# Attention and a gated feed-forward layer on one core: how the first exponentials are turned, who copies the early results, and where the first matmul groups end

## The chip, the cores and the metric

The program runs on one core of one Trainium2 chip. The metric is the device time of an execution in microseconds (us). The kernel before took 466.61 us, the median of three executions (465.33 to 467.41). One more execution was profiled; the profile, its page and every stretch quoted here are of that one.

## The reference

Twelve heads of eight batches, 448 positions of 64 values: a softmax with one more term in its denominator, then a dense layer with Mish between two matrices.

```python
scores = (1 / sqrt(64)) * q @ k.transpose(0, 1, 3, 2)        # 8 x 12 x 448 x 448
m = max(scores, axis=-1)
e = exp(scores - m)
attn = e / (sum(e, axis=-1) + exp(-m) + 1e-09)
x = (attn @ v) as rows of 12 * 64 = 768 values                # 3584 rows
h = x @ w_in                                                  # 768 x 2048
g = h * tanh(log1p(exp(h)))                                   # Mish
out = g @ w_out                                               # 2048 x 768
```

## The kernel before, in words

Two heads make a pair; 8 batches of 6 pairs are 48 pairs, numbered from 0. For a pair, `load_pair` (L133) brings q, k and v, `cast` (L177) makes them bf16 on GpSimd, `transpose_pair` (L207) turns q and k on TensorE into a PSUM bank, and `evac_qk` (L238) copies them to SBUF. `scores` (L309) multiplies in four steps; after each step VectorE takes the negated row maxima (L350, `negm`), and `exps` (L355) lets ScalarE write the exponentials with their sums (L366, `en`). For the second product the exponentials must be turned, `en` to `eT`. `normalise` (L428) issues that as a transposing DMA on SyncE (L440), called T(p) below for pair p. It is cut in four blocks j along the key positions. `turn_on_pe` (L445) turns one block with seven TensorE transposes (L452) and a VectorE copy (L455). `av_pair` (L463) multiplies by v (L480), AV(p) below, and its `evac` copies the result to `xT` (L493 or L495).

The division by the denominator is done in one of two ways. For a pair that `divided` (L108) names, `normalise` multiplies `en` on VectorE by the reciprocal, seven instructions (L432), ahead of T(p). For the others `spread_rden` (L396) spreads the reciprocals over a PSUM bank with 16 small matmuls (L411), a copy makes `rb` of it (L420), and the output is multiplied by it as it leaves PSUM (L495).

The head of the program (L656) does pairs 0 to 5 one after another; pair p's AV follows three pairs later. Then come units of three pairs, u = 2 to 17 (u = 2 is pairs 6 to 8, u = 3 is 9 to 11, u = 4 is 12 to 14, u = 5 is 15 to 17), with two more units without attention at the end. A unit has twelve steps, in which AVs of earlier pairs and parts of the second matrix product (`mm2_part`, L588) are woven between the scores, and then eight passes f = 0 to 7 that do the first matrix product (`mm1_mish`, L532; matmuls L525, Mish L541), turn later q and k, and issue the T of the unit's three pairs in the order of the list `todo` (L784).

Which groups of L525 start early is written out: in u = 2 and 3 `mm1_begin` (L513) starts four groups in the steps; in u = 2 they stop short of the last one or two matmuls, which `mm1_mish` adds in its pass. Pairs 5, 6 and 7 (`BY_PE`, L633) are turned by TensorE wholly and have no T.

All order is by hand; each engine takes its instructions strictly in program order. Four orders matter here. SyncE's queue holds the loads (L140), the T, the turns of later q and k (L202) and the stores (L553). GpSimd's holds the casts and, at L174, the weights' loads: `load_w` (L165) first copies a few values of some pair's `eT` (L169), so it waits until that pair's T has landed: six pieces of `w_in` behind T(4), five pieces behind T(8), four behind the last pair in u = 3. Two PSUM banks, `mo`, are shared by everything that calls `mo_take` (L124). And `flush_late` (L120) puts copies out of PSUM where the next step begins. `eT` has three buffers, so T(p) waits for AV(p-3).

Of the kernel before, what the change touches and what calls it, by code (L numbers as in the profile page):

```python
# [15 lines left out]
UNIT_PAIRS = 3  # L16
# [3 lines left out]
def kernel(  # L20
# [9 lines left out]
    nc = tc.nc  # L30

    B, H, S, D = q.shape
# [3 lines left out]
    NT = 4  # L36
    SP_ = S // NT
    HP = H // 2
    DM_T = d_model // 128
# [5 lines left out]
    FF_U = FF_T // UNITS_PER_B  # L45
# [57 lines left out]
    QB = S // 64  # L103
    DIAG_FROM = 2 * HP
    LATE_DIV = 2 * HP
    EARLY_DIV = (HP, HP + 1, HP + UNIT_PAIRS)

    def divided(p):  # L108
        return p >= LATE_DIV or p in EARLY_DIV
# [10 lines left out]
    def flush_late():  # L120
        while late:
            late.popleft()()
# [42 lines left out]
    def load_w(n, behind=None):  # L165
        if behind is not None:
            i = n_marks[0]
            n_marks[0] += 1
            nc.gpsimd.tensor_copy(  # L169
                out=marks[0:1, i, 0:2], in_=att[behind]["eT"][0:1, NT - 2, 2 * S - 2 : 2 * S]  # L170
            )
        for _ in range(min(n, len(pieces))):
            dst, src = pieces.popleft()
            nc.gpsimd.dma_start(out=dst, in_=src.rearrange("(a p) c -> p a c", p=128))  # L174
# [253 lines left out]
    def normalise(p, dma=True):  # L428
        st = att[p]
        en = st["en"]  # L430
        for i in range(NTILE if divided(p) else 0):
            nc.vector.tensor_scalar(  # L432
                out=en[:, :, i, 0:SP_], in0=en[:, :, i, 0:SP_],
                scalar1=st["rden"][:, i : i + 1], scalar2=None, op0=ALU.mult,
            )
        eT = eT_pool.tile([128, NT, 2 * S], BF16, tag="eT", name="eT")
        st["eT"] = eT
        if dma:
            n = NT - 1 if p < HEAD else NT
            nc.sync.dma_start_transpose(  # L440
                out=eT[:, 0:n, :].rearrange("c j (i q) -> c (j i) q", q=128),
                in_=en[:, 0:n].rearrange("q j i c -> q (j i c)"),
            )

    def turn_on_pe(p, j, busy_first=0):  # L445

        st = att[p]
        own = mo_take()
        keep_busy(busy_first, bank=own)
        ps = own[:, :].bitcast(BF16).rearrange("c (i q) -> c i q", q=128)  # L450
        for i in range(NTILE):
            nc.tensor.transpose(ps[0:SP_, i, :], st["en"][:, j, i, 0:SP_], ident)  # L452

        def evac():
            nc.vector.tensor_copy(  # L455
                out=st["eT"][0:SP_, j, :].rearrange("c (i q) -> c i q", q=128),
                in_=ps[0:SP_, 0:NTILE, :],
            )
            mo_free.append(own)

        late.append(evac)

    def av_pair(p, bank=None, beside=None, half=None, hold=False):  # L463
        b, hp = p // HP, p % HP
        eT = att[p]["eT"]
        v_bf = casted[p]["v"]
        if b not in xT:
            xT[b] = xT_pool.tile([128, DM_T, S], BF16, tag="xT", name="xT")
        if half is not None:
            bank = free_half(half)  # L470
            mms = av_beside.setdefault(half * STEPS + STEPS - 1, [])
        av = mo_take() if bank is None else bank
        for j in range(NT):
            for h in range(2):
                if p >= DIAG_FROM:
                    by_h = eT[0:SP_, j, :].rearrange("c (i h r) -> c h i r", h=2, r=64)
                    e_h = by_h[:, h]
                else:
                    e_h = eT[0:SP_, j, h * S : (h + 1) * S]
                mm = nc.tensor.matmul(  # L480
                    av[h * 64 : (h + 1) * 64, 0:S],
                    lhsT=v_bf[:, h, j * D : (j + 1) * D],
                    rhs=e_h,
                    start=(j == 0), stop=(j == NT - 1),
                )
                if half is not None:
                    apart(mm, half_max[half])
                    mms.append(mm)

        def evac():  # L490
            to = xT[b][:, hp, :]
            if divided(p):
                read = nc.vector.tensor_copy(out=to, in_=av[:, 0:S])  # L493
            else:
                read = nc.vector.tensor_tensor(  # L495
                    out=to, in0=av[:, 0:S], in1=rb.pop(p), op=ALU.mult
                )
            if half in half_exp:
                apart(read, half_exp[half])
            elif beside is not None or half is not None:  # L500
                av_read[beside if half is None else half * STEPS + STEPS - 1] = read
            if bank is None:
                mo_free.append(av)

        if p in spread_copy:
            late.append(spread_copy.pop(p))
        (held if hold else late).append(evac)
        del att[p], casted[p], qkT[p]


    begun = {}

    def mm1_begin(b, ff, upto):  # L513

        bank = mm1_bank(ff)
        begun[b, ff] = (bank, upto)
        mm1(b, ff, bank, 0, upto)

    def mm1_bank(ff, ahead=2):
        at = ff % FF_U - 2  # L520
# [2 lines left out]
    def mm1(b, ff, bank, lo, hi):  # L523
        for dm in range(lo, hi):
            nc.tensor.matmul(  # L525
                bank[:, 0:S],
                lhsT=w_in_sb[:, dm, ff * 128 : (ff + 1) * 128],
                rhs=xT[b][:, dm, :],
                start=(dm == 0), stop=(dm == DM_T - 1),
            )  # L530
# [99 lines left out]
    HEAD = HP  # L630
    BY_DMA_FROM = 2 * HP + 2 * UNIT_PAIRS

    BY_PE = {HEAD - 1: 1, HEAD: -2, HEAD + 1: 2}  # L633
    AV_AT = {0: {1: 3, 5: 4, 8: 5}, 1: {1: 8, 4: 6, 8: 7}}
    RDEN_AT = {0: {0: 3, 2: 4, 5: 5}, 1: {0: 8}, 2: {3: 10, 5: 11}}
    MM1_AT, MM1_SHORT = (6, 7, 9, 10), (2, 1, 1, 1)

    W_AT = ({5: 2}, {1: 3})
# [17 lines left out]
    for p in range(HEAD):  # L656
        for s in range(STEPS):
            exps(p * STEPS + s)
            if s == 0 and p == 0:
                evac_qk(1, act=True)  # L660
            flush_late()
            if s == 1:
                late.extend(held)
                held.clear()
                flush_late()
            if s == 2:
                evac_qk(p + 2, act=p % 2 == 0)
            scores_ahead(HEAD * STEPS + 3)
            if s == 0:
                transpose_pair(p + 2)  # L670
                if p:
                    denominators(p - 1)
            if s == 1 and p:
                turn_on_pe(p - 1, NT - 1)
            if s == 2:
                if p >= 3:
                    spread_rden(p - 3)
                cast(p + 3, "qkv" if p + 3 < HEAD else "qk")
                if p == HEAD - 1:
                    load_w(6, behind=p - 1)  # L680
            if s == 3:
                if p >= 3:
                    av_pair(p - 3, hold=True)
                if p + 5 < 10:
                    load_pair(p + 5, "qkv" if p + 5 <= HEAD else "qk")
                normalise(p, dma=p not in BY_PE)
            if s < 3:
                keep_busy(2, half=p)
    denominators(HEAD - 1)

    for u in range(UNITS_PER_B, N_UNITS + 2 * UNITS_PER_B):
# [5 lines left out]
        p0 = u * UNIT_PAIRS  # L697
        if attn and u >= first_mm2:
            av_with.update({p0 + i: p0 + i - UNIT_PAIRS for i in range(UNIT_PAIRS)})
        nxt = p0 + UNIT_PAIRS  # L700
        end = min(nxt, N_PAIRS) * STEPS

        for n in range(steps):
            pi, s = divmod(n, STEPS)
            p, idx = p0 + pi, p0 * STEPS + n
# [46 lines left out]
            for pe, n0 in BY_PE.items():  # L752
                j = n - n0
# [29 lines left out]
        b, w = (u - UNITS_PER_B) // UNITS_PER_B, u % UNITS_PER_B  # L783
        todo = sorted(range(p0, nxt), key=lambda p: p in BY_PE)  # L784
        if u == UNITS_PER_B + 1:
            todo = [p0 + 1, p0, p0 + 2]
        for f in range(FF_U):
            if moe:
                mm1_mish(b, w * FF_U + f)
            if u == UNITS_PER_B and f == 3:  # L790
                load_w(5, behind=p0 + 2)
            if u == UNITS_PER_B + 1 and f == FF_U - 1:
                load_w(4, behind=p0 + 2)
            if not attn:
                continue
            if f == 0:
                denominators(p0, UNIT_PAIRS)
                for p in todo[:2] if p0 < LATE_DIV else todo[:1]:
                    normalise(p, dma=p not in BY_PE)
            if f in (1, 3, 5):  # L800
                if nxt < BY_DMA_FROM:
                    transpose_pair(nxt + f // 2, bank=f // 2 % 2)
                    evac_qk(nxt + f // 2)
            if f == 1 and p0 < LATE_DIV:
                normalise(todo[2], dma=todo[2] not in BY_PE)
            if f == FF_U - 1:
                scores_ahead(min(nxt * STEPS + len(sc_tiles), N_PAIRS * STEPS))
            if f in (3, 5) and p0 >= LATE_DIV:
                p = todo[1 + f // 5]
                normalise(p, dma=p not in BY_PE)  # L810
    flush_late()
# [31 lines left out]
```

## Time and profile before

| | |
|---|---|
| median of three executions | 466.61 us |
| profiled execution, device time | 465.31 us |
| its span, first to last instruction | 463.5 us |
| mean granted TensorE clock | 0.993 |
| TensorE matmuls busy | 443.5 us, 96% |
| VectorE busy | 346.9 us, 75% |
| ScalarE busy | 331.4 us, 72% |
| GpSimd busy | 184.3 us, 40% |
| DMA moved | 97.93 MB, mean 211 GB/s |

The page cuts the span into 40 equal slices and gives each engine's busy share as a digit; a second part follows the chain of work that ended last; a third lists groups of instructions with the busy time, the mean of one, and the idle time before them with what ended it. "<-" reads "made from" in a name and "released by" after an idle time. Stretches give the busy time of each engine between two moments, then the granted clock, the DMA engines' busy share (above 1 where packets of two queues are under way on the same engine) and the rate. A DMA's time to landing counts from its issue to its last write.

### The profile page before, as it was taken

To read this page: it belongs to the slowest core of one execution; us is meant where nothing else is said; L and a number is where in the kernel's file an instruction comes from. 1 tells how busy PE (TensorE), PEld (TensorE's weight loads), DVE (VectorE), ACT (ScalarE), POOL (GpSimd) and SP (SyncE) were. 2 spreads that over 40 slices of the span, in tenths; PEclk is the share of its full clock that TensorE was granted. 3 is DMA by queue.
4 is the path that set the end of the run, shared out by engine and by line. 5 is a ranking of instruction groups with operands and counts; after the bars stand their busy time and mean duration, and the time that the engine had idled before them with its cause. 6 is when DMAs were issued, how large, how long until landed. Compare 5 with 4: busy or idle time off the path is not lost.

```text
span 463.5 us, 8735 instructions
## 1 busy us (share of the span) xinstructions
PE 443.5 (96%) x2991; PEld 243.9 (53%) x2991; DVE 346.9 (75%) x670; ACT 331.4 (72%) x874; POOL 184.3 (40%) x267
## 2 busy tenths in 40 slices
PE   6788989999999999999999999999999999999996
PEld 3344555555555555555555555555555555556563
DVE  5989969688798898989898979989888979311021
ACT  5999878898797878787887968787878779221300
POOL 4434648043346271736464643727363610100000
PEclk9989999999999999999999999999999999999999
DMA  8999999999999999999989999999999392911122
GB/s 245 243 213 233 223 215 229 190 238 246 235 262 275 239 252 218 283 211 263 256 275 242 267 219 231 260 231 247 258 272 235 113 243 76 245 62 35 34 69 68
DMA packets 232492, 97.93 MB, mean 211 GB/s; under 512 B 189312, under 2 KB 228992, under 8 KB 232448
## 3 DMA queue, kind: packets, MB, share of 16 engines
q1 hardware_dynamic: 224928, 91.06, 83.1%
q0 software_dynamic: 7488, 6.29, 8.6%
q8 instruction: 23, 0.38, 0.3%
q14 instruction: 21, 0.17, 0.1%
q10 hardware_dynamic: 32, 0.02, 0.0%
HBM read 45.61 MB, written 11.01 MB: 122 GB/s over the span
## 4 chain that ended last, share of the span: by engine, by line
PE 71%; ACT 14%; DVE 11%; issue 2%; DMA 0%; SPq 0%; DVEq 0%; ACTq 0%
PE mo L525 26%; PE mo L588 24%; ACT en L366 11%; DVE negm L350 8%; PE sc L329 8%; PE sc L480 6%; PE sc L525 4%; PE sc L290 1%; DVE eT L455 1%; PE sc L335 1%; DVE xT L493 1%; PE mo L480 1%; ACT L541 1%; PE sc L225 1%; ACT kT_all L280 0%
## 5 line engine op out<-in xcount | busy, mean ns | idle before, releaser
L366 ACT ACTIVATE en<-sc,negm 128x448 bf16<-128x448 f32 x336 | 209.3, 640 | 29.7 <-DVE negm L350 28.0
L350 DVE TENSOR_REDUCE negm<-sc 128x2 f32<-128x896 f32 x192 | 180.4, 969 | 42.3 <-PE sc L329 32.0
L588 PE MATMUL mo<-w_out_sb,gT 128*128 128x384 bf16 (+1 forms) x1024 | 166.7, 306 | 0.4 <-DVE rb L420 0.4
L525 PE MATMUL mo<-xT,w_in_sb 128*128 128x448 bf16 x660 | 132.2, 352 | 1.0 <-ACT gT L541 0.5
L588 PEld LDWEIGHTS <-gT 128*128 128x128 bf16 x1024 | 96.3, 98 | 56.0 <-issue 1.9
L270 POOL TENSOR_SCALAR qd<-qT_all 64x448 bf16<-64x448 bf16 x60 | 79.8, 1330 | 90.4 <-DMA qT_all<-q_cast 61.9
L525 PEld LDWEIGHTS <-w_in_sb 128*128 128x128 bf16 x768 | 74.2, 98 | 69.7 <-issue 3.9
L541 ACT ACTIVATE gT<-mo 128x448 bf16<-128x448 f32 x110 | 58.2, 543 | 68.9 <-PE mo L525 68.7
L432 DVE TENSOR_SCALAR en<-en,rden 128x448 bf16<-128x448 bf16 x273 | 87.1, 394 | 0.6
L366 ACT ACTIVATION_READ_ACCUMULATOR en<-sc,negm 128x1 f32 x336 | 71.0, 211 | 0.0
L571 DVE COPY o_sb<-mo 128x384 f32<-128x384 f32 (+1 forms) x64 | 31.9, 498 | 49.8 <-PE mo L588 49.0
L329 PE MATMUL sc<-kT_all,qd 128*128 128x448 bf16 x252 | 67.6, 354 | 0.0
L480 PE MATMUL sc<-eT,v_bf 112*64 112x448 bf16 x336 | 39.8, 357 | 1.6 <-ACT en L366 1.1
L329 PEld LDWEIGHTS <-qd 128*128 128x128 bf16 x252 | 24.6, 98 | 28.7 <-issue 12.9
L191 POOL CAST q_cast<-q_f 112x512 bf16<-112x512 f32 x47 | 28.7, 610 | 5.5 <-DMA q_f<-in_q_dram 5.4
L480 PEld LDWEIGHTS <-v_bf 112*64 112x64 bf16 x384 | 20.1, 109 | 20.1 <-issue 12.6
L191 POOL CAST k_cast<-k_f 112x512 bf16<-112x512 f32 x47 | 28.6, 609 | 0.7 <-DMA k_f<-in_k_dram 0.4
L191 POOL CAST v_bf<-v_f 112x512 bf16<-112x512 f32 x48 | 28.1, 607 | 1.3 <-DMA v_f<-in_v_dram 0.9
L735 POOL COPY marks<-en 1x2 bf16<-1x2 bf16 x12 | 2.1, 174 | 64.2 <-DVE en L432 64.2
L525 PE MATMUL sc<-xT,w_in_sb 128*128 128x448 bf16 x108 | 23.4, 353 | 1.4 <-ACT gT L541 1.4
L493 DVE CAST xT<-sc 128x448 bf16<-128x448 f32 x36 | 22.1, 615 | 0.0
L541 ACT ACT_TABLE_LOAD x14 | 18.0, 1283 | 0.8 <-PE mo L525 0.6
(63 smaller groups left out, 238.8 us busy)
## 6 DMA issues: line engine op xcount, KB each, us to landing
k_f<-in_k_dram SPq DMA_DIRECT2D x48, 224.0 KB, 5.1
q_f<-in_q_dram SPq DMA_DIRECT2D x48, 224.0 KB, 4.9
v_f<-in_v_dram SPq DMA_DIRECT2D x48, 224.0 KB, 5.0
w_in_sb<-in_moe_w_in_dram POOLq DMA_DIRECT2D x12, 256.0 KB, 9.8
w_out_sb<-in_moe_w_out_dram POOLq DMA_DIRECT2D x8, 384.0 KB, 13.7
out_dram<-o_sb SPq DMA_DIRECT2D x7, 336.0 KB, 3.4
out_dram<-o_sb SPq DMA_DIRECT2D x8, 288.0 KB, 4.8
out_dram<-o_sb SPq DMA_DIRECT2D x8, 240.0 KB, 3.4
```

The costliest lines, as they stand in the source:

```text
L191: nc.gpsimd.tensor_copy(out=to[nm], in_=src)
L270: q_reads.append(by.tensor_scalar(out=qd[rows, :, h, :], in0=q_ps[rows, 0:S].rearrange("d (i r) -> d i r", i=QB), scalar1=SCALE, scalar2=N ...
L329: nc.tensor.matmul(sc[:, bk, 0:S], lhsT=qT[:, i].rearrange("d h r -> d (h r)"), rhs=kT, start=True, stop=True,)
L350: half_max[p] = nc.vector.tensor_reduce(out=negm, in_=sc[:, 0 : len(cols), 0:S], axis=AX.X, op=ALU.max, negate=True)
L366: e = nc.scalar.activation(out=st["en"][:, :, c, 0:SP_], in_=sc[:, bk, 0:S].rearrange("q (j c) -> q j c", j=NT), func=AF.Exp, bias=st["neg ...
L432: nc.vector.tensor_scalar(out=en[:, :, i, 0:SP_], in0=en[:, :, i, 0:SP_], scalar1=st["rden"][:, i : i + 1], scalar2=None, op0=ALU.mult,)
L480: mm = nc.tensor.matmul(av[h * 64 : (h + 1) * 64, 0:S], lhsT=v_bf[:, h, j * D : (j + 1) * D], rhs=e_h, start=(j == 0), stop=(j == NT - 1),)
L493: read = nc.vector.tensor_copy(out=to, in_=av[:, 0:S])
L525: nc.tensor.matmul(bank[:, 0:S], lhsT=w_in_sb[:, dm, ff * 128 : (ff + 1) * 128], rhs=xT[b][:, dm, :], start=(dm == 0), stop=(dm == DM_T - 1),)
L541: nc.scalar.activation(out=gT[:, ff, b % 2 * S : b % 2 * S + S], in_=h_ps[:, 0:S], func=AF.Mish)
L571: nc.vector.tensor_copy(out=o_sb[:, cols.start : cols.start + n_dve], in_=st["o"][:, 0:n_dve])
L588: nc.tensor.matmul(st["o"][:, 0:n_cols], lhsT=gT[:, ff, i * 128 : (i + 1) * 128], rhs=w_out_sb[:, ff, cols], start=(ff == 0), stop=(ff == ...
```

## The change

1. T(0) to T(4) turn all four blocks; before they turned three, and the fourth was turned by TensorE and copied by VectorE (`turn_on_pe` at L674 goes).
2. In the head, q and k of pairs 2, 4 and 6 are copied from PSUM by VectorE (L263, L278) and no longer by ScalarE (L261, L280).
3. Pair 10 joins the divided pairs: its `en` is multiplied ahead of T(10), its `spread_rden` in u = 4 goes, its output is copied plainly. With that u = 3 issues T(11), T(9), T(10) where it issued T(10), T(9), T(11), and the weights' loads at the end of u = 3 wait for T(10), again the last.
4. The outputs of pairs 6 and 7 are copied from PSUM by ScalarE, in u = 3.
5. Before the eight passes of a unit all started groups of L525 are ended (`mm1_finish`); this moves instructions in u = 2 alone.
6. In u = 4 the third pair's multiplication and T, those of pair 14, move from pass 5 to pass 7, behind the next unit's first scores.

```diff
-    EARLY_DIV = (HP, HP + 1, HP + UNIT_PAIRS)
+    EARLY_DIV = (HP, HP + 1, HP + UNIT_PAIRS, HP + UNIT_PAIRS + 1)
...
-            n = NT - 1 if p < HEAD else NT
             nc.sync.dma_start_transpose(
-                out=eT[:, 0:n, :].rearrange("c j (i q) -> c (j i) q", q=128),
-                in_=en[:, 0:n].rearrange("q j i c -> q (j i c)"),
+                out=eT.rearrange("c j (i q) -> c (j i) q", q=128),
+                in_=en.rearrange("q j i c -> q (j i c)"),
             )
...
             if divided(p):
-                read = nc.vector.tensor_copy(out=to, in_=av[:, 0:S])
+                read = (nc.scalar.copy if p in BY_PE else nc.vector.tensor_copy)(out=to, in_=av[:, 0:S])
...
+    def mm1_finish():
+
+        flush_late()
+        for (b, ff), (bank, lo) in list(begun.items()):
+            mm1(b, ff, bank, lo, DM_T)
+            begun[b, ff] = (bank, DM_T)
...
-    RDEN_AT = {0: {0: 3, 2: 4, 5: 5}, 1: {0: 8}, 2: {3: 10, 5: 11}}
+    RDEN_AT = {0: {0: 3, 2: 4, 5: 5}, 1: {0: 8}, 2: {5: 11}}
...
             if s == 2:
-                evac_qk(p + 2, act=p % 2 == 0)
+                evac_qk(p + 2)
...
-            if s == 1 and p:
-                turn_on_pe(p - 1, NT - 1)
...
         if u == UNITS_PER_B + 1:
-            todo = [p0 + 1, p0, p0 + 2]
+            todo = [p0 + 2, p0, p0 + 1]
+        mm1_finish()
...
             if u == UNITS_PER_B + 1 and f == FF_U - 1:
-                load_w(4, behind=p0 + 2)
+                load_w(4, behind=p0 + 1)
...
-            if f in (3, 5) and p0 >= LATE_DIV:
+            third = 5 if nxt >= BY_DMA_FROM else FF_U - 1
+            if f in (3, third) and p0 >= LATE_DIV:
                 p = todo[1 + f // 5]
                 normalise(p, dma=p not in BY_PE)
```

## The prediction

> **What bounds the kernel now.** I read the page's slices and chain first, then stretches around the changed places, then the queues of SyncE and TensorE, and last single transposes with their time to landing.
>
> The slices and the engines' shares in the chain:
>
> ```profile
> DMA  8999999999999999999989999999999392911122
> PE 71%; ACT 14%; DVE 11%; issue 2%; DMA 0%; SPq 0%; DVEq 0%; ACTq 0%
> ```
>
> The chain names engines and no DMA, but the DMA row is at 9 from the second slice to the thirtieth, past 345 us. The 71% of TensorE are almost all behind 110 us, where no edit is. In front of that the edits meet ScalarE and VectorE, so stretches there (columns: length, busy time of PE, PEld, DVE, ACT and POOL, granted clock, DMA share, GB/s):
>
> ```profile
> 23.07:26.49 3.42, 1.83 (x17) 1.00 (x16) 3.05 (x6) 3.42 (x13) 0.71 (x2) 1.00 1.00 240
> 26.49:29.90 3.41, 3.41 (x27) 1.74 (x28) 2.94 (x6) 3.06 (x11) 1.50 (x4) 0.50 1.18 244
> 32.00:33.00 1.00, 1.00 (x14) 0.60 (x12) 0.87 (x4) 0.88 (x3) 0.00 (x0) 1.00 0.09 31
> 38.00:39.00 1.00, 1.00 (x12) 0.43 (x9) 0.97 (x4) 1.00 (x3) 0.00 (x0) 1.00 0.32 76
> 85.50:96.00 10.50, 9.96 (x74) 5.73 (x73) 7.59 (x18) 9.29 (x19) 0.52 (x2) 1.00 1.29 215
> ```
>
> In the head ScalarE is full, VectorE nearly. The DMA engines have two holes there, near 32 and 38 us, while SyncE waits for AV(0) and AV(1) to free an `eT` buffer. From 42 us to 96 I find none of more than half a microsecond.
>
> TensorE's order around u = 4's first AV, its queue's wait before that, T(9) itself, and T(10) to T(11) on SyncE:
>
> ```profile
> 93.50 2.44 PE L588 MATMUL mo<-w_out_sb,gT 128*128 128x384 bf16 x14
> 95.93 0.95 PE L480 MATMUL sc<-eT,v_bf 112*64 112x448 bf16 x8
> ...
> L480 PEldq EVENT_SEMAPHORE  x5: 51/51/51, 95.8 to 131.9; - x5
> ...
> L440 SPq DMA_TRANSPOSE eT<-en x1: 3931/3931/3931, 89.8 to 89.8; - x1
> DMA to landing us min/median/max: 6.0/6.0/6.0
> ...
> 79.56 17.95 SPq L440 DMA_TRANSPOSE eT<-en  x3
> ```
>
> This pair of numbers carries the forecast: T(9) lands at 89.8 + 6.0 = 95.8 us and AV(9) starts at 95.93. Everything ahead may become 4 us faster; if T(9) isn't earlier, TensorE waits at AV(9), and all later work stands behind it in program order. The next such place is the same: T(12), issued at 112.4, takes 11.1 to land, 123.5, and AV(12) starts at 123.64. T(15) lands at 148.4 (140.7 + 7.7) for an AV at 148.94.
>
> **The change part by part.** Durations below are spacings in the timeline of the profiled execution, which took 465.31 us, 1.30 under the median.
>
> Head, edits 1 and 2. ScalarE loses three pairs of copies of 0.43 + 0.42: 2.55. VectorE loses five `eT` copies at a spacing of 0.53, 2.65, and gains three pairs of copies of 0.30 + 0.30, 1.80: net -0.85. TensorE loses five times seven transposes, 0.39 each time and 0.92 once at half clock. The first of the moved copies helps nothing, since it stands between two row maxima that ScalarE waits for at 14 us. The ScalarE idle of 0.60 at 19.77 goes too. I take 2.5 (bounds 1.0 and 3.5) by the start of u = 2.
>
> Edit 5: in u = 2 TensorE waited 1.37 at 61.35 for Mish to leave the PSUM tile in whose other half its last started group ended. With the groups ended before, that wait goes: -1.4. Late next is the bank for the fifth group, free after the first Mish at 60.0, before TensorE gets there.
>
> Edit 4: VectorE, 9.76 of 10 busy at 70 to 80 us, loses two copies of 0.53: -1.06. ScalarE takes 2 x 0.43 in gaps of 0.76 and 1.17 that it has there.
>
> Edit 3: seven multiplications, 1.81, in the passes of u = 3; VectorE is idle there for 1.30 and 1.41, which hides them; without that cover 1.8. In u = 4 one L411 group of 0.64 and one `rb` copy of 0.53 go, but ScalarE sets the pace from 99.93 to 104.3, so I take -0.3 (bounds 0 and -1.2).
>
> Edit 6: the first scores of u = 5 are in PSUM by 118.95, their maximum started at 119.22 behind the 1.81 of multiplications: -0.3. T(14)'s data are then ready at about 123.9, still before SyncE reaches it at 124.87; GpSimd's mark and casts behind it (119.25 to 123.3) move 4.7 later, up to SyncE's next turn at 128.59: cost 0, and 0.5 without that cover.
>
> So the engines' own work would bring AV(9) forward by about 3.8, after what u = 2 takes back below.
>
> Now the queue. T(0) to T(4) grow by a third. Back to back T(9) and T(11) land at 95.8 and 99.1 (93.9 + 5.2), so 28 blocks cost 3.3, seven cost 0.82, five times that 4.1 us of DMA time. The bounds: nothing, if the holes swallow it, and 4.1. Worked through: T(2), landing at 30.8 (25.2 + 5.7), comes three steps later, 33.2; the loads behind it end 2.0 after it as before, 35.2; the hole at 32 is gone, so T(3) at 38.5; two loads at 0.7 each, the spacing in which the first loads land; T(4) at 43.2, where it was 42.4 (37.6 + 4.8). T(4) is 0.7 late, and with it the six `w_in` pieces that GpSimd holds back for it. The first three land at 50.4, 51.8 and 53.4, against matmuls that start at 53.38; with the head 2.5 faster they'd be wanted from 50.9 on, and come at 51.1 to 54.1. This takes back 1.3: 2.5 - 1.3 + 1.4 + 1.06 gives 3.7, with roundings the 3.8 above.
>
> From T(4) to T(9) the DMA engines stay full, so T(9) carries the 0.7 on, with two corrections. T(8) now meets more of `w_in` under way: +0.3 (bounds 0 and 1). T(10) took 12.3 to land among the `w_out` pieces where T(11) behind it took 5.2; T(11), now first and issued near 81.7 with the end of the unit, meets less of them: -0.7 (bounds 0 and -2.7). Sum for T(9): +0.3, landing at 96.1; AV(9) starts 0.3 later than before and TensorE stands about 4 us before it. In u = 4 edit 3 gives -0.3, but T(12) lies behind loads and weights that are as late as T(10), third now, so AV(12) is at about +0.3 again and edit 6's 0.3 is waited away. Later units have 0.5 to 2 us between landing and AV and keep what they get. Total: 465.31 + 0.3 = 465.6 as a profiled execution, 466.9 against the median. The profile shows no later place that could give back.
>
> The Trainium skill (DMA: Bandwidth & Descriptors, Issuing engines are not separate DMA queues) says that DMAs started by different engines run on the same 16 DMA engines and interleave. The trace agrees (12.3 beside GpSimd's loads, 5.2 without), and by it a gain ahead of T(9) can't pass while the weights move.
>
> **The rivals.**
>
> Gains pass. T(11) is late enough that `w_out` runs alone to its end, and the mixing that made 12.3 out of 5.2 is saved in full: T(9) at 95.8 + 0.7 - 2.7 = 93.8, -2.1 at AV(9), u = 4 -0.6 more: 465.3 - 2.7 = 462.6, or 463.9 against the median; were T(9) no bound at all, -4.4 and 462.2. I take 463.4. For it: at 80 to 82 us GpSimd's queue has the engines nearly alone and yet moves only some 200 GB/s. Against it: T(11) is issued some 5 us before the pieces end.
>
> The clock. TensorE now stands for about 4 us before AV(9). Above, 1.83 busy of 3.42 was followed by a stretch at clock 0.50, 3.41 long. A stretch boundary every 3.41 us from 26.49 falls on 91.3 and 94.7; TensorE would be busy 0.8 in that one, and half speed would hold to 98.2, from AV(9) at 96.1 on: 2.1 us of it, some 1.0 lost: 466.6, or 467.9. It decides if the wait is over about 2 us. [...]
>
> Slower. The larger transposes' 4.1 land wholly behind: T(4) at 46.5, `w_in`, T(8), `w_out` and T(9) all as late, AV(9) at 99.7 and T(12) the same, +3.8: 469.1, or 470.4. For it: T(0), T(1) and T(2), issued among loads, took 4.0, 4.8 and 3.6 to issue where T(3) took 2.8, so a third more may cost more than 0.82. Against it: the two holes. It decides when T(4) lands later than about 45.
>
> That an edit doesn't do what it says is excluded by the built order of instructions: each moves as told.
>
> **How the numbers follow.** About 0.5%, 2.3 us, is what a measurement of this kernel tells from no change: 464.3 to 468.9. The forecast has 0.42, its own range 465.3 to 468.5; gains pass 0.25; the clock 0.14; slower 0.19. Faster: 0.22 of "gains pass" and 0.02 of the forecast, 0.24. Slower: 0.17 of the last rival, 0.06 of the clock together with a late T(9), 0.05 of the forecast, 0.28. Same: 0.48. The range leaves out the better third of "gains pass" and the worse half of "slower": 463.0 to 469.6.
>
> **What would show it.** T(4) landing near 43.2 and the first `w_in` matmul near 53; the 1.37 wait at Mish gone; a TensorE wait of 3 to 5 us for `eT` ahead of the first AV of u = 4, T(9) landing at 95 to 97; the clock digit right after. Wrong would be: T(9) landing below 94 (gains pass), or T(4) above 45 (slower), or an AV in a later unit that waits for its T.

## The result, and the profile after

The changed kernel took 472.65 us, the median of six executions (470.37 to 474.06), against 467.01 for the kernel before beside it: a ratio of 1.0108, with a 95% interval of 1.0081 to 1.0136. It became slower by 5 to 6 us, outside the range that I had given. The profiled execution took 471.79 us (span 470.0), 6.5 more than that of before. Two of the twelve executions of run 11 below were in a slower state and are left out of its numbers.

Three numbers say how: AV(3) starts 3.5 us earlier than before, AV(5) 2.1 later, AV(9) 4.1 later. The gain in the head came, and more than it was lost between pairs 3 and 5.

In u = 3 the AVs stand in the order AV(8), AV(6), AV(7). The expectations quoted below, where they give a start of one of these or its difference to before, count by place: their AV(6) is the first of the three, pair 8's, and their AV(8) the last, pair 7's. The text keeps to the pairs.

The slices of the changed kernel and the shares of its chain:

```profile
DMA  8999999999999999999999999999999493921122
PE 71%; ACT 9%; DVE 9%; DMA 5%; issue 3%; POOL 1%; SPq 0%; DVEq 0%; ACTq 0%; POOLq 0%
```

DMA, which stood at 0% of the chain, now has 5% of it. The five stretches of the prediction (columns as there):

```profile
23.07:26.49 3.42, 2.34 (x18) 1.11 (x17) 3.33 (x7) 3.35 (x12) 0.90 (x4) 1.00 1.14 250
26.49:29.90 3.41, 3.16 (x38) 1.55 (x38) 3.23 (x5) 3.41 (x13) 1.07 (x2) 1.00 1.18 201
32.00:33.00 1.00, 1.00 (x20) 0.50 (x18) 1.00 (x3) 0.54 (x4) 0.81 (x2) 1.00 0.79 250
38.00:39.00 1.00, 1.00 (x8) 0.35 (x9) 1.00 (x2) 1.00 (x5) 0.00 (x0) 1.00 1.11 331
85.50:96.00 10.50, 9.38 (x70) 5.00 (x69) 7.13 (x24) 8.56 (x21) 0.52 (x2) 1.00 0.99 166
```

The two holes of the DMA engines are filled: 250 and 331 GB/s where 31 and 76 had been. But a hole stands elsewhere now. From 40 to 42 us, while T(4) is under way, the engines move less than 100 GB/s:

```profile
40.00:41.00 1.00, 0.91 (x18) 0.59 (x17) 0.90 (x5) 1.00 (x4) 0.00 (x0) 1.00 2.09 86
41.00:42.00 1.00, 0.38 (x6) 0.34 (x5) 1.00 (x3) 1.00 (x5) 0.00 (x0) 1.00 0.47 99
```

The kernel before had one slow microsecond in its T(4), at a full DMA share:

```profile
39.00:40.00 1.00, 0.59 (x10) 0.57 (x9) 1.00 (x2) 0.96 (x5) 0.89 (x4) 1.00 1.27 101
```

T(4) is late. SyncE's transpose of pair 4, who waited for it, and its time to landing:

```profile
L439 SPq DMA_TRANSPOSE eT<-en x1: 5457/5457/5457, 36.7 to 36.7; - x1
...
  POOL marks L169: 6.4, 1
...
DMA to landing us min/median/max: 7.5/7.5/7.5
```

Issued 0.9 earlier than before, it lands at 44.1 and not at 42.5, and GpSimd stands 6.4 us at the copy that waits for it (1.90 before). What follows is in TensorE's timeline of the changed kernel:

```profile
49.12 0.93 PE L411 MATMUL mo<-ident,hl 128*64 128x128 bf16 x16 [0.97 <-POOL hl L391]
49.98 0.95 PE L479 MATMUL sc<-eT,v_bf 112*64 112x448 bf16 x8
...
52.26 0.93 PE L531 MATMUL mo<-xT,w_in_sb 128*128 128x448 bf16 x2 [1.03 <-DMA w_in_sb<-in_moe_w_in_dram]
53.57 0.93 PE L531 MATMUL mo<-xT,w_in_sb 128*128 128x448 bf16 x2 [0.38 <-DMA w_in_sb<-in_moe_w_in_dram]
...
57.01 0.55 PE L531 MATMUL mo<-xT,w_in_sb 128*128 128x448 bf16 x1 [0.42 <-DMA w_in_sb<-in_moe_w_in_dram]
```

Here are four waits that the kernel before didn't have. The first is not for the weights but for the reciprocals of pair 5 (`hl`), a GpSimd instruction that stands in its queue behind the mark and the six weight loads; the others are for the pieces of `w_in`. They add up to 2.8 us, and the clock falls behind them. Stretches of the same kernel:

```profile
48.08:51.50 3.42, 2.14 (x28) 1.02 (x26) 2.17 (x4) 2.07 (x6) 3.33 (x8) 1.00 1.05 205
51.50:54.90 3.40, 2.26 (x6) 0.37 (x6) 1.09 (x2) 1.76 (x6) 3.40 (x7) 0.50 1.21 222
54.90:58.30 3.40, 2.98 (x11) 0.84 (x11) 1.20 (x2) 1.34 (x4) 0.93 (x2) 0.50 1.18 246
58.30:61.70 3.40, 3.40 (x14) 1.25 (x11) 2.33 (x7) 2.12 (x4) 0.42 (x2) 0.50 1.23 219
```

For 10.2 us TensorE runs at half clock, though it stood still for no more than 1.03 us at a time. Then u = 3, on ScalarE:

```profile
81.04 0.53 ACT L492 CAST xT<-sc 128x448 bf16<-128x448 f32 x1 [1.31 <-DVE negm L350]
...
87.23 0.53 ACT L492 CAST xT<-sc 128x448 bf16<-128x448 f32 x1 [1.34 <-PE sc L479]
```

These are the moved copies of edit 4. ScalarE waits 1.3 before each, with the exponentials behind it. AV(7), which stands behind the first of them, is 1.1 later against before than AV(6) was. Around AV(9), on TensorE, and SyncE's T(11) and T(9) ahead of it:

```profile
97.70 2.44 PE L594 MATMUL mo<-w_out_sb,gT 128*128 128x384 bf16 x14
100.07 0.95 PE L479 MATMUL sc<-eT,v_bf 112*64 112x448 bf16 x8
```

```profile
L439 SPq DMA_TRANSPOSE eT<-en x2: 3807/3928/4050, 89.8 to 93.9; - x2
...
DMA to landing us min/median/max: 5.3/5.7/6.2
```

T(9) lands at 93.9 + 5.3 = 99.2, 3.4 later than before, and AV(9) starts at 100.07 with no wait ahead of it: queue and engines are late by about the same. The last part is at u = 6:

```profile
155.47 0.95 PE L479 MATMUL sc<-eT,v_bf 112*64 112x448 bf16 x8 [2.91 <-DMA eT<-en]
```

T(15) was issued at 145.1 and landed at 155.3; TensorE stood 2.91 for it. From there the difference stays at 6.2 to 6.5.

### The profile page after: what moved, and what is told of

Same layout as the page of the kernel before. It is cut to its first block, busy times and chain, and to the rows that moved or that the text cites. A ratio compares the mean times of both kernels' runs of the same rounds, so it can differ in the third digit from the quotient of the medians.

```text
span 470.0 us, 8633 instructions
## 1 busy us (share of the span) xinstructions
PE 445.6 (95%) x2940; PEld 241.5 (51%) x2940; DVE 348.0 (74%) x675; ACT 329.6 (70%) x870; POOL 184.3 (39%) x267
## 4 chain that ended last, share of the span: by engine, by line
PE 71%; ACT 9%; DVE 9%; DMA 5%; issue 3%; POOL 1%; SPq 0%; DVEq 0%; ACTq 0%; POOLq 0%
PE mo L531 26%; PE mo L594 24%; ACT en L366 8%; PE sc L329 7%; DVE negm L350 6%; PE sc L479 6%; PE sc L531 4%; DMA w_in_sb<-in_moe_w_in_dram 2%; DMA eT<-en 2%; DVE xT L492 1%; DMA qT_all<-q_cast 1%; PE sc L290 1%; PE sc L335 1%; PE sc L225 1%; PE mo L479 1%
## 5 line engine op out<-in xcount | busy, mean ns | idle before, releaser
L531 PE MATMUL mo<-xT,w_in_sb 128*128 128x448 bf16 x660 | 134.2, 355 | 3.4 <-DMA w_in_sb<-in_moe_w_in_dram 1.8
L432 DVE TENSOR_SCALAR en<-en,rden 128x448 bf16<-128x448 bf16 x280 | 91.2, 402 | 0.6
```

What stands on the lines that cost most here:

```text
L432: nc.vector.tensor_scalar(out=en[:, :, i, 0:SP_], in0=en[:, :, i, 0:SP_], scalar1=st["rden"][:, i : i + 1], scalar2=None, op0=ALU.mult,)
L531: nc.tensor.matmul(bank[:, 0:S], lhsT=w_in_sb[:, dm, ff * 128 : (ff + 1) * 128], rhs=xT[b][:, dm, :], start=(dm == 0), stop=(dm == DM_T - 1),)
```

## The experiments

Each kernel was executed six to twelve times. Ratios are against the kernel before measured beside it (its medians were 466.8 to 467.6). The other columns: the mean granted clock over the kernel's timed executions, and from one profiled execution of each the landing of T(4), T(8), the last of the four `w_out` pieces that load in u = 2 and 3, and T(9), and the start of AV(9) against before.

| kernel | median us | ratio, 95% interval | clock | T(4) | T(8) | w_out | T(9) | AV(9) |
|---|---|---|---|---|---|---|---|---|
| before | 467 | 1 | 0.990 | 42.5 | 65.1 | 89.3 | 95.8 | 0 |
| changed | 472.65 | 1.0108, 1.0081 to 1.0136 | 0.983 | 44.1 | 68.0 | 92.7 | 99.2 | +4.1 |
| 1 without edit 1 | 464.32 | 0.9942, 0.9919 to 0.9965 | 0.994 | 41.6 | 66.7 | 90.2 | 96.8 | +1.0 |
| 2 edit 1 alone | 471.26 | 1.0089, 1.0062 to 1.0115 | 0.982 | 46.5 | 69.7 | 93.8 | 101.5 | +5.7 |
| 3 edit 1's cost alone | 470.13 | 1.0068, 1.0042 to 1.0094 | 0.988 | 44.9 | 68.2 | 94.8 | 100.7 | +5.0 |
| 4 edit 1's gain alone | 468.48 | 1.0024, 0.9998 to 1.0049 | 0.983 | 43.1 | 65.9 | 92.9 | 98.5 | +2.7 |
| 5 T(4) short | 470.35 | 1.0069, 1.0035 to 1.0102 | 0.985 | 45.6 | 68.4 | 92.6 | 99.1 | +3.5 |
| 6 weights sooner | 474.76 | 1.0200, 1.0151 to 1.0249 | 0.983 | 47.7 | 75.9 | 97.7 | 103.9 | +8.1 |
| 7 one wait filled | 468.81 | 1.0033, 1.0006 to 1.0060 | 0.991 | 46.2 | 70.8 | 93.7 | 100.4 | +4.8 |
| 8 both waits filled | 469.32 | 1.0052, 1.0020 to 1.0084 | 0.992 | 45.2 | 69.0 | 91.9 | 98.5 | +2.7 |
| 9 without edit 4 | 470.11 | 1.0050, 1.0026 to 1.0075 | 0.984 | 46.6 | 69.4 | 92.9 | 99.3 | +3.5 |
| 10 edit 4 alone | 466.47 | 0.9979, 0.9957 to 1.0000 | 0.990 | 41.2 | 65.3 | 89.3 | 96.1 | +1.1 |
| 11 without 1 and 4 | 465.16 | 0.9956, 0.9930 to 0.9982 | 0.992 | 41.7 | 67.1 | 89.6 | 96.1 | +0.3 |
| 12 edits 2 and 5 alone | 466.11 | 0.9978, 0.9954 to 1.0003 | 0.990 | 41.0 | 64.6 | 90.3 | 95.7 | -0.1 |
| 13 as 1, held last | 467.80 | 1.0024, 1.0005 to 1.0043 | 0.992 | 42.4 | 68.7 | 89.6 | 99.3 | +3.5 |
| 14 as 4, held last | 469.12 | 1.0053, 1.0032 to 1.0075 | 0.982 | 40.3 | 63.7 | 87.6 | 98.0 | +2.2 |
| 15 as 1, held second | 465.30 | 0.9972, 0.9942 to 1.0001 | 0.991 | 41.4 | 65.8 | 89.3 | 96.1 | +0.3 |
| 16 as 4, held second | 465.60 | 0.9948, 0.9921 to 0.9974 | 0.988 | 44.1 | 66.3 | 89.0 | 96.5 | +0.7 |

A profiled execution lies up to 4 us from its kernel's median (run 13: 471.80 against 467.80), so columns from a trace tell where, and the medians how much.

**1. The changed kernel with edit 1 undone: three blocks by DMA, the fourth on TensorE.**

```diff
+            n = NT - 1 if p < HEAD else NT
-                out=eT.rearrange("c j (i q) -> c (j i) q", q=128),
+                out=eT[:, 0:n, :].rearrange("c j (i q) -> c (j i) q", q=128),
...
+            if s == 1 and p:
+                turn_on_pe(p - 1, NT - 1)
```

> The changed kernel with its first edit undone: T(0) to T(4) turn three blocks again, TensorE and VectorE the fourth; all other edits stay. Theory late weights (the larger transposes delay T(4), the w_in pieces held behind it come after TensorE wants them, and TensorE's wait drops the clock): T(4) lands near 42.5 or earlier, the waits for w_in (1.0, 0.4 and 0.4 us) are below 0.5 in sum, no half clock between 51 and 62 us; some 4.5 to 6 us back, ratio to before 0.996 to 1.002. Rival idle TensorE (the head's missing transposes alone let the clock drop) says the same for this run. Rival blocked ScalarE (the loss is the copies of outputs 6 and 7 that wait for AV(6) and AV(7) ahead of exponentials): ratio stays at 1.007 or above.

464.32 us: edit 1 is the loss. The other five edits alone make the kernel faster, by 0.35 to 0.81%, so this version is faster than both kernels. AV(8) is 3.0 earlier than before, with no wait for `w_in` and no half clock in u = 2. At AV(9) its profiled execution shows the wait that the forecast had put there:

```profile
PE sc L480 <- DMA eT<-en: 2.1, 1, 2.1
```

**2. Edit 1 alone, on the kernel before.** The diff is the reverse of the one above.

> The kernel before with the first edit alone: four blocks by DMA for pairs 0 to 4. Late weights: T(4) at 43.5 to 44.5, first w_in pieces at 51.5 to 53.5; the head is faster by only about 1.5 us, so TensorE waits 0.5 to 1.5 us less than in the changed kernel; with or without a half clock the ratio is 1.002 to 1.010. Blocked ScalarE: 0.995 to 1.000, since VectorE and TensorE have less to do and no copy is moved.

471.26, +0.9%. T(4) lands at 46.5 and AV(5) starts 4.4 later than before, with 2.0 of waits for `w_in`, 2.0 for `hl`, and the clock at half from 53.5 to 60.3. So edit 1 needs none of the other edits to lose; on top of them it costs more (464.3 to 472.65).

**3. The cost of edit 1 without its gain.**

```diff
-            n = NT - 1 if p < HEAD else NT
+            n = NT
...
-                turn_on_pe(p - 1, NT - 1)
+                turn_on_pe(p - 1, NT - 1, out=spare)
```

> The cost of edit 1 without its gain: the kernel before, where the transposes of the head take all four blocks, while TensorE and VectorE still turn the fourth block as before, into a spare place. Edit 1 whole, on the kernel before, gave 471.3 (T(4) 46.5, first w_in piece 54.9, AV(5) +4.4, end +5.1). 'Volume' (a third more DMA time per transpose lands behind): the same T(4) at 46 to 47, AV(5) at +5 to +6, median 471 to 473. 'Bunching' (it is the engines' gain that puts transposes and loads on top of each other): T(4) near 43.2 as I had worked out, AV(5) +1, median 468.

470.13: the longer transposes cost some 3 us by themselves. T(4) lies between the two expectations, at 44.9, and AV(5) at +1.3, so at this place "bunching" is not refuted: with engines that come no earlier, TensorE waits only 1.7 for `w_in`, and there is no half clock in u = 2. The rest is lost later. T(10), issued at 80.7, takes 17.0 to land, and at AV(9) stands

```profile
PE sc L484 <- DMA eT<-en: 3.8, 1, 3.8
```

**4. The gain without the cost.** Three blocks by DMA and nobody turns the fourth; AV of pairs 0 to 4 reads the third twice, so the fourth block's share is missing from the output.

```diff
-            if s == 1 and p:
-                turn_on_pe(p - 1, NT - 1)
...
-                    e_h = eT[0:SP_, j, h * S : (h + 1) * S]
+                    e_h = eT[0:SP_, min(j, NT - 2) if p < HEAD - 1 else j, h * S : (h + 1) * S]
```

> The gain of edit 1 without its cost: the kernel before, where the transposes of the head take three blocks as before and nobody turns the fourth; AV of pairs 0 to 4 reads the third block a second time instead, so the fourth block's part of the scores is left out of the output. 'Volume': AV(3) -2, T(4) at 41 or earlier, first w_in piece near 49, no wait for w_in, AV(6) -2, AV(9) bound by T(9) at about 0, median 466 to 467. 'Bunching': T(4) past 43.5, waits for w_in and the half clock in u = 2 as with edit 1 whole, median 469 to 471.

468.48: no gain, rather a loss (the interval just takes in 1). All AVs from pair 3 to pair 8 are 2.3 earlier than before, as "volume" said, with nothing lost in u = 2. Then all of it and more goes at AV(9), which neither theory had. TensorE, and two stretches ahead of it:

```profile
98.62 1.71 PE L480 MATMUL sc<-eT,v_bf 112*64 112x448 bf16 x8 [4.98 <-DMA eT<-en]
```

```profile
84.00:88.00 4.00, 3.46 (x34) 2.15 (x32) 3.07 (x11) 3.99 (x9) 0.41 (x2) 1.00 1.35 193
88.00:92.00 4.00, 4.00 (x23) 2.13 (x22) 2.13 (x4) 2.83 (x5) 0.00 (x0) 1.00 1.26 95
```

From 88 to 92 us the DMA engines are as busy as ever (1.26) and move 95 GB/s. T(10), which the faster engines issued at 77.3 (79.6 before), takes 17.4 to land beside the `w_out` pieces, and these end at 92.9 (89.3 before). That made a new question: does a transpose among weight loads slow the whole stretch (runs 13 to 16)?

**5. T(4) alone back to three blocks.**

```diff
+            n = NT - 1 if p == HEAD - 2 else NT
...
+            if s == 1 and p == HEAD - 1:
+                turn_on_pe(p - 1, NT - 1)
```

> The changed kernel with T(4) alone back to three blocks, its fourth turned by TensorE; T(0) to T(3) stay whole. 'T(4) is the link' (its own length is what delays the mark on GpSimd, hl and the weights): T(4) about 1 to 2 earlier, at 42.5 to 43.5, w_in first at 50.5 to 51.5, AV(6) -1 to -2 against the changed kernel, median 470. 'Whole volume' (T(0) to T(3) have already pushed the queue): T(4) at 43.5 or later, median within 1 of 472.6.

470.35, T(4) at 45.6. The trace speaks for "whole volume": the short T(4) takes 6.2 to land and not 7.5, but it lands no earlier, since T(3) had landed 2.7 later than in the changed kernel. That is one execution of each. The median is 2.3 under the changed kernel's, and the intervals overlap; as much as that may be TensorE's seven transposes that fill time, or nothing.

**6. The weights held behind T(3) instead of T(4).**

```diff
-                    load_w(6, behind=p - 1)
+                    load_w(6, behind=p - 2)
```

> The changed kernel with the six w_in pieces held behind T(3) in place of T(4); every engine's order is the same. Late weights: GpSimd issues them near 38 us, the first three land by 50, TensorE's wait for w_in goes and with it the half clock at 51 to 62 us; T(4) may land 1 to 3 us later, which AV(4) at 50 bears; 4 to 6 us back, ratio 0.996 to 1.003. Idle TensorE: the wait goes, but half clock stays for some 3 to 10 us: ratio 1.003 to 1.007. If the sum of DMA work alone sets T(9): ratio above 1.006, with T(9) at 98 or later.

474.76, the slowest of all. Neither theory holds; of the three cases only the last fits (ratio above 1.006, T(9) at 98 or later: 1.0200 and 103.9), and by far more than it says. The pieces come in time (47.5, 49.0, 51.1), AV(5) is 3.9 earlier than before, and then T(8) is issued at 54.2 with weight pieces 7 and 8 right behind it. SyncE, and stretches:

```profile
54.23 15.60 SPq L439 DMA_TRANSPOSE eT<-en  x1
```

```profile
60.00:64.00 4.00, 4.00 (x30) 2.01 (x29) 2.64 (x6) 2.81 (x5) 0.04 (x1) 1.00 1.15 104
64.00:68.00 4.00, 3.06 (x41) 2.26 (x40) 3.76 (x7) 4.00 (x13) 0.00 (x0) 1.00 1.37 82
```

The issue alone takes 15.6, the landing 21.7 (6.9 before), at 82 to 104 GB/s, and TensorE stands 7.5 for it at AV(8). Weights that were asked for sooner made this transpose three times as long.

**7 and 8. Dummy matmuls where TensorE waits.** Run 7 put five ahead of pair 4's reciprocals, which was the wrong place, since the wait is for pair 5's, and seven ahead of the first `w_in` group; run 8 eight at pair 5's and the same seven.

```diff
         begun[b, ff] = (bank, upto)
+        if ff == 0:
+            keep_busy(7, bank=bank)
...
+                    busy_first=8 if spread[n] == 5 else 0,
```

> The changed kernel with dummy matmuls ahead of two places where TensorE waited in u = 2: five ahead of the wait for pair 4's reciprocals at 49.1, seven ahead of the first w_in group at 52.3. Nothing else differs. In the changed kernel the clock was 0.50 from 51.5 to 61.7. 'Idle TensorE' (the waits are short, the half clock behind them is what costs): clock 1.00 in those stretches, AV(5) at about 56 instead of 58.0, AV(6) at about 73.7 instead of 75.7, and the end some 2 us earlier than in the changed kernel: span 468, median 470.5. 'Late weights' (the third w_in piece at 57.0 sets the pace whatever the clock): AV(5) and AV(6) within 0.5 of the changed kernel, span 470, median 472.5.

> The changed kernel with dummy matmuls at both waits: eight ahead of pair 5's reciprocals (the wait for GpSimd's hl, which stands behind the six weight pieces it issues) and seven ahead of the first w_in group. 'Idle TensorE': no half clock between 48 and 62, AV(5) at -0 to -1 against before plus what T(4) is late, AV(6) 2 us sooner than in the changed kernel, median 469 to 470. 'Late weights': the matmuls only take the place of the wait, AV(6) as in the changed kernel, median 472.5.

468.81 and 469.32: work added and time saved, 3.8 and 3.3 us by the medians, 3.5 and 2.6 by the ratios (run 7's interval is apart from the changed kernel's, run 8's just touches it). In run 8's trace the stretch that was at 0.50 is at 1.00:

```profile
51.50:54.90 3.40, 2.68 (x18) 1.04 (x15) 1.62 (x2) 2.70 (x9) 3.40 (x7) 1.00 1.24 221
```

Run 7's profiled execution still had half clock from 50.8 to 57.6, but over all its executions the mean clock is 0.991 as in run 8 (0.992), where the changed kernel has 0.983. Half clock for x us lowers the mean by x / 2 over the span, so by estimate these are 9 and 8 us at half clock in place of 16.5 (2 x 0.0175 x 471), and half of the difference is about the 3 to 4 us. By medians and mean clocks "idle TensorE" holds. The path to the end is not shown: AV(8) of run 8 is 1.8 earlier than in the changed kernel, but at AV(14) the two profiled executions are equally late (3.6 us each), and they end apart only by the wait for T(15). The remainder, 0.3 to 0.5% over before, fits "late weights": run 8 has T(9) at 98.5.

**9 and 10. Edit 4.** The changed kernel with VectorE copying the outputs of pairs 6 and 7 again, and the kernel before with edit 4 alone.

```diff
-                read = (nc.scalar.copy if p in BY_PE else nc.vector.tensor_copy)(out=to, in_=av[:, 0:S])
+                read = nc.vector.tensor_copy(out=to, in_=av[:, 0:S])
```

> The changed kernel with the outputs of pairs 6 and 7 copied by VectorE again, nothing else. Blocked ScalarE: the waits of ScalarE for AV(7) (1.34 us) and of TensorE for ScalarE (1.32 us) in u = 3 go, 1 to 2 us back: ratio 1.006 to 1.009. The forecast's step (the copies relieve a full VectorE, 1.06 us): 1.012 to 1.014. If u = 3 gains but T(9) or T(12) is the bound: 1.0108 as measured.

> The kernel before with edit 4 alone: two xT copies on ScalarE instead of VectorE. 'Blocked ScalarE' (in order, the copy waits for the AV matmuls, and the exponentials behind it wait with it): AV(8) +1.2, T(9) issued and landed about 1 later, end +1, median 468.5. My forecast's term (ScalarE takes them in gaps, VectorE is relieved): AV(8) -1.0, T(9) bound as before, median 467.5 or a little under.

Without edit 4 the difference to before stays at +1.0 through all three AVs of u = 3; with it alone it grows by 1.1 between AV(6) and AV(7). ScalarE's waits in run 10 between 76 and 92 us:

```profile
ACT xT L493 <- PE sc L480: 1.3, 1, 1.3
ACT xT L493 <- DVE negm L350: 1.3, 1, 1.3
```

So "blocked ScalarE" is right about u = 3. About the end the runs disagree. In the changed kernel edit 4 costs 0.5% (472.65 against 470.11, intervals apart). Alone it costs nothing (0.9957 to 1.0000), and where edit 1 is left out, run 1 has it and run 11 below doesn't, with no difference clear of the noise. Why it costs only beside edit 1 is not shown; a bound at AV(9) doesn't explain it, for in run 10 the delay passes AV(9) (+1.1, with T(9) at 96.1; 0.6 of it is gone again at AV(12)), and run 9 stands 2.5 at AV(9) without the edit.

**11 and 12. The rest in parts.** Edits 2, 3, 5 and 6, and edits 2 and 5.

> The changed kernel with edits 1 (whole turns by DMA) and 4 (xT copies on ScalarE) undone; with edit 1 alone undone it took 464.3, AV(6) -3.0, AV(8) -1.8, AV(9) +1.0 behind T(9) landing at 96.8. 'Blocked ScalarE' (the copies cost u = 3 1.2 us and delay the issue of the next transposes): AV(8) at -3.0 or better, T(11) issued some 1 us earlier than 84.5, T(9) landing near 95.8, span 464, median 463.2. 'Pinned by the queue' (T(9) lands when the w_out pieces let it, whatever the engines do): AV(8) better but T(9) at 96.8 again, TensorE waiting 3 for it, median 464.3.

> The kernel before with edits 2 (VectorE copies q and k in the head) and 5 (groups ended ahead of Mish) alone; the order of pairs 9 to 11 stays as before, T(9) first. These two gave -1.4 and -1.6 by AV(6) where edit 1 was undone. 'Pinned by the queue': T(9) lands at 95 to 96 beside the w_out pieces, issued earlier and taking longer, so AV(9) within 0.7 of before and median 467. 'Gains pass' (T(9) first in the queue comes with the engines): T(9) at about 93.5, AV(9) at -2.3 and the end the same, median 465.2.

465.16 and 466.11, from each other and from run 1 not to be told apart. Both have the AVs of u = 3 2.2 to 2.6 earlier than before, and both give it back at T(9), at 96.1 and 95.7 where it was 95.8: "pinned by the queue". T(10) in run 12, issued at 76.9 in place of 79.6, lands at 92.4 in place of 91.9. How far edits 3 and 6 help is open; they were not run alone.

**13 to 16. The first transpose of u = 3 held until weight pieces have landed.** SyncE sends a transfer of 4 bytes that reads a `w_out` piece ahead of the transpose, and so waits for that piece: the last of the four in 13 and 14, the second in 15 and 16. Runs 13 and 15 are run 1 with this, 14 and 16 are run 4, with the same part of the output missing.

```diff
+        if p == HP + UNIT_PAIRS + 1:
+            nc.sync.dma_start(out=marks[0:1, 3, 4:6], in_=w_out_sb[0:1, 4, 0:2])
         if dma:
```

> The changed kernel with edit 1 undone (464.3), and the first transpose of u = 3, T(11), held on SyncE's queue behind a 4-byte transfer that reads the last of the four w_out pieces; without the hold T(11) was issued at 84.5, amid those pieces, which ended at 90.2, and landed at 93.5, T(9) at 96.8. 'Mixing' (a transpose among weight loads slows both): the pieces end at 87 to 88, T(11) lands 4 to 5 later, T(9) at 94 to 95.5, AV(9) -0.5 to -1.5 against before, median 462.5. 'Bytes' (the DMA engines have the same work in any order): T(9) at 97 or, by the turnaround of the queue, 98 to 99, median 464.5 to 466.

> The kernel with the gain of edit 1 without its cost (468.5, with the fourth block left out of the output), and T(10), the first transpose of u = 3, held behind the last of the four w_out pieces. Without the hold T(10) was issued at 77.3 and took 17.3 to land, the pieces ended at 92.9, T(9) landed at 98.5 and TensorE waited 5.0. 'Mixing': the pieces end at 87 to 88.5, T(9) at 94.5 to 96, AV(9) at -1 to 0, median 465.5 to 466.5. 'Bytes': T(9) at 98 or later, median 468.5.

Behind the last piece it lost 3.5 us on run 1 (467.80, intervals apart) and gained nothing on run 4 (469.12). The expectation for run 13 names the cause under "bytes", the turnaround of the queue. Run 14:

```profile
84.00:86.00 2.00, 1.46 (x21) 1.11 (x19) 1.97 (x9) 1.99 (x4) 0.52 (x2) 1.00 0.45 70
86.00:88.00 2.00, 2.00 (x15) 1.08 (x14) 1.49 (x5) 2.00 (x5) 0.00 (x0) 1.00 0.05 8
88.00:90.00 2.00, 2.00 (x18) 1.17 (x16) 0.78 (x2) 1.44 (x4) 0.00 (x0) 1.00 0.15 36
90.00:92.00 2.00, 2.00 (x13) 1.05 (x12) 0.94 (x1) 1.39 (x3) 0.00 (x0) 1.00 1.28 290
```

The pieces ended 5.3 us sooner than in run 4 (3.2 counted from T(8)), as mixing has it, but from 84 to 90 us little moved: the last piece came in slowly until 87.6, T(10) was issued at 88.5, and its data flowed from about 89.7. The hold gave the gain back.

> As the hold behind the last w_out piece on the changed kernel without edit 1, but T(11) waits for the second of the four pieces only, which landed 3.4 earlier there. With the hold behind the last piece the pieces' data stopped near 88 and the first data of T(11) moved near 91, so some 3 us of the hold were an empty queue. 'Mixing' with that turnaround taken out: T(11) starts moving as the pieces end, lands at 92, T(9) at 95.5, AV(9) at -0.5, median 463 to 464. 'Bytes': T(9) at 96.8 as without the hold, median 464.5 to 465.5.

> The gain of edit 1 alone, T(10) held behind the second of the four w_out pieces. Held behind the last, the pieces landed at 87.6 in place of 92.9, the DMA engines then moved next to nothing from 85 to 90, and T(9) came at 98.0. 'Mixing': the pieces end near 88, T(10) lands at 91 to 92, T(9) at 95 to 96, TensorE's wait for it falls from 5.0 to 2 or 3, median 466 to 467. 'Bytes': T(9) at 98, median 468.5.

Behind the second piece the empty stretch is gone. Run 16, the same two stretches as shown of run 4, and its AV(9):

```profile
84.00:88.00 4.00, 3.46 (x31) 2.10 (x29) 3.75 (x13) 3.97 (x9) 0.52 (x2) 1.00 1.32 177
88.00:92.00 4.00, 4.00 (x29) 2.25 (x27) 1.30 (x3) 2.83 (x7) 0.00 (x0) 1.00 1.09 236
```

```profile
96.62 0.95 PE L482 MATMUL sc<-eT,v_bf 112*64 112x448 bf16 x8 [2.15 <-DMA eT<-en]
```

236 GB/s for 95, a wait of 2.15 for 4.98, and 465.60 for 468.48, with intervals apart (0.9921 to 0.9974 against 0.9998 to 1.0049): the transpose was issued 8.7 us later and landed 2.3 earlier. Mixing is shown for a T issued early. In run 15 the same hold gains nothing (465.30 against 464.32 of run 1, intervals overlapping): there T(11) was issued at 84.5 without it and at 86.2 with it.

## Why the prediction was wrong, step by step

- **The head, 2.5 (1.0 to 3.5).** The mechanism held and the size was at its bound: AV(3) is 3.5 earlier.
- **T(4) at 43.2, "the hole at 32 is gone".** This is the step that failed. I let two holes take up 3.4 of the 4.1 us that the blocks add. The holes were filled at their places, and T(3) landed at 37.6, even before the 38.5 of my sum. But T(4) landed 6.6 behind it, where I had 4.7, and in that time a hole stood, from 40 to 42 us. T(4) itself took 7.5 to land in place of 4.8, of which a third more data explains 1.6 by proportion. I had looked for holes in the DMA share alone; at a full share the rate shows others. Why this one came is open. One execution is not the rule: in the six with edit 1 whole (changed, 2, 3, 7, 8, 9) T(4) landed at 44.1 to 46.6, median 45.7, in the ten without (before, 1, 4, 10 to 16) at 40.3 to 44.1, median 41.65. That is about 4.1 later: my upper bound, and the case of the last rival. (Runs 5 and 6 change T(4) or the weights behind it.)
- **`w_in`, "this takes back 1.3".** The first three pieces came at 52.2, 53.5 and 57.0 and not by 54.1; TensorE waited 1.8 for them. And I had not named what stands behind them on GpSimd: the six loads take 4.54 us to issue, and pair 5's reciprocals and the next casts queue behind the mark and the loads. That is 0.97 of TensorE in the changed kernel, 2.0 in run 2.
- **The clock.** I had it as a rival of 0.14 and at AV(9). In the changed kernel it came 45 us earlier, at the `w_in` waits, and by the medians it is about half of the loss: runs 7 and 8 take 2.6 to 3.8 us of 5.6 off by filling waits. At AV(9) it came too, wherever TensorE stood there for long: of the ten profiled executions with a wait of 2 us or more (runs 1, 3, 4, 6, 9, 11 to 14 and 16) eight have half clock at it or right behind it (not 11 and 13), and there AV(10) is another 1.0 to 2.4 later.
- **What half clock followed.** The Trainium skill (TensorE: Matmul & The Clock Gate, HAM oscillation — how this bites in real kernels) gives the rule that idle gaps should stay under about 3.4 us. The trace differs: no gap was over 1.03, and half clock lasted 10.2; before, no gap from 23.07 to 26.49 us was over 0.96, and half clock followed. Busy time does better, though not as a sharp threshold. The clock changes at steps of 3.41 us. Of the stretches between its steps at full clock, in all eighteen profiled executions, the 14 in which TensorE was busy for less than 1.65 us were all followed by half clock and none above 2.19 was; of the 48 in between, half were. The 2.14 of the changed kernel was, 2.15 in run 8 was not.
- **Edit 5, -1.4.** Right where the clock is whole: AV(8), the next one, against AV(5) gains 1.5 in runs 1, 11 and 12. In the changed kernel the Mish wait of 1.37 is gone too, and the half clock took its place.
- **Edit 4, -1.06 on VectorE with ScalarE's copies "in gaps".** Wrong in sign: +1.1 at AV(7). A gap in an in-order queue is not free time: the copies waited 1.3 each (by the profile one for the AV that it reads, the other for a row maximum), and the exponentials that stood behind the gap came after them. A copy took 0.53, not 0.43.
- **T(9) +0.3 at 96.1.** It was +3.4. That T(9) hangs on the chain of weights more than on the engines was right: in all eighteen profiled executions it lands 52 to 58 us after T(4), with T(8), the `w_out` pieces and the first T of u = 3 as the links between, and engines 2 us ahead did not bring it forward (runs 4, 11, 12). But the chain is not stiff: of the 3.4 in the changed kernel 1.7 stand at T(4), 3.0 at T(8) (I had 1.0 there) and 3.4 at the last piece. The correction of -0.7 for T(11) was no help either.
- **"TensorE waits 4 us at AV(9)".** Not in the changed kernel, whose engines had lost as much by then; in runs 1 to 4, 6, 9 and 11 to 16, yes (1.5 to 5.0).
- **u = 4, -0.6 by edits 3 and 6.** AV(11) to AV(14) gain 0.6. Runs 3, 4 and 10, which have neither edit, gain the same, so this is not theirs.
- **"No later place".** In the profiled execution T(15) cost 2.9. Other runs show at most some 0.9 there, so it is not settled whether this is a rule of the changed kernel. At AV(12), which I had named as the next such place, runs 5, 7, 11 to 13 and 15 wait 0.7 to 2.6 for T(12).

Of the rivals, "slower" with 470.4 came nearest: AV(9) at 99.7 was 100.07, and its mechanism was right. Its sign, T(4) later than 45, was met in four of the six executions with edit 1 whole, though not in the changed kernel's own (44.1), and it lacked the clock.

## To carry to other kernels

Work given to busy DMA engines is not hidden by short holes, which may only move: count all of it until a trace shows otherwise, and follow what hangs on the last transfer, also the instructions that queue behind the waiting mark. A faster engine that issues a transpose sooner into weight loads can get it later; the rate of a stretch at full DMA share (95 against 236 GB/s) shows it. And before a copy is moved into another engine's gap, ask what it must wait for there.

## What the runs showed of the hardware

- A transpose beside GpSimd's weight loads moved, together with them, 82 to 104 GB/s in its slowest stretches (runs 4 and 6) at a DMA share of 1.15 to 1.37; the weight pieces alone moved 198 (run 13, 86 to 88 us), with plain loads beside them 240 (before, 76 to 80 us), and transposes one behind the other about 290. The Trainium skill (DMA: Bandwidth & Descriptors, Issuing engines are not separate DMA queues) has them interleave on the same engines; the runs agree, and add that the sum falls to about half.
- A transfer held for another's landing left the DMA engines nearly empty: 8 GB/s from 86 to 88 us and 36 from 88 to 90, with the landing at 87.6, the issue at 88.5 and data from about 89.7 (run 14).
- Four waits of 0.4 to 1.0 us within 8 us went with 10.2 us of half clock; twelve to fifteen needless matmuls saved some 3 us.
